# Seven block products instead of eight for five projections of the second attention, in a kernel of four fused layers

## The chip, the cores and the metric

One core of one Trainium2 chip runs the whole program. Its engines work side by side, each through its own list of instructions in order: TensorE (PE) multiplies, VectorE (DVE), ScalarE (ACT) and GpSimd (POOL) work element by element, SyncE (SP) issues DMAs. The metric is the device time of one execution in microseconds. Before the change the median of three runs was 269.13 (268.15 to 269.72).

## The reference, cut to what matters

Four layers follow one another on a sequence of 2048 tokens with 512 features: a linear attention, a feed-forward, and the same two again with the same weights. Each works on the layer norm of the running sum x and is added to it.

```python
def _A_ref(x, wqkv, wo):            # H = 32 heads of 16
    q, k, v = split(x @ wqkv)
    phi = lambda t: jnp.where(t > 0, t + 1, jnp.exp(t)) + 1e-6
    pq, pk = phi(q), phi(k)
    kv = einsum("bhsd,bhse->bhde", pk, v); z = einsum("bhsd->bhd", pk)
    o = einsum("bhqd,bhde->bhqe", pq, kv) / (einsum("bhqd,bhd->bhq", pq, z) + 1e-6)
    return o @ wo
def _B_ref(x, w1, w2):              # 512 -> 1376 -> 512
    return maximum(x @ w1, 0) @ w2
x = x + _A_ref(_layernorm(x), A_wqkv, A_wo)
x = x + _B_ref(_layernorm(x), B_w1, B_w2)
x = x + _A_ref(_layernorm(x), A_wqkv, A_wo)
x = x + _B_ref(_layernorm(x), B_w1, B_w2)
```

## The kernel before, in words

The 2048 tokens are 16 tiles of 128, in four chunks of four tiles. The running sum lies in xres, a tile's normalised rows in xn, their transposes (features down the partitions) in Tb. The transposes of the first six tiles are made on TensorE, all others by DMA, two tiles at a time (tr0_0 is the first half of chunk 0).

The program is written as a graph of named operations, each with its engine, what it reads and writes and a planned cost. `_list_schedule` puts them in an order per engine. An operation's priority is its place in the program plus an entry of the table HINTS; an entry with "!" fixes which of two engines does a flexible operation. The prefix is the layer (0 and 2 the attentions, 1 and 3 the feed-forwards). The table was found by a search, so layers overlap: the second attention's first chunks are worked on while the first feed-forward's last chunks still run. Every engine then follows its list in order and waits on semaphores.

**Attention.** For each chunk, K is computed in rows of tokens (`a_k`, kproj: four products of 128x512 per tile) and Q in rows of features (`a_q`, qproj: four products of 128x512 for each 128 features). So one chunk of either takes 16 products of 512 columns. `phi_evac` (lines 635 to 654) evicts each: on ScalarE a linear part with bias 1 + 1e-6 (_lin, L643) and an exponential (_exp, L645), both from PSUM, and on VectorE a minimum with 1 (_em, L647) and a maximum of the two parts (_phi, L653). `a_g` multiplies phi(K) with xn (g0, g1), `a_kv` with the V weights (kv), `a_m` masks by head (kvmask, L739) and multiplies with wo (m0 to m3), which ScalarE or VectorE evicts to Mf (mev0 to mev3, L746). The denominators go through `a_den`, logarithm and exponential, and a DMA that spreads them (spread); pqs (L801) applies them. The output tiles are Q times Mf (fin; the first four in two halves), added to xres by resid (L667) with the row sums, and sq (L675) gives the squares. A chain on GpSimd (mean, variance, power, L580 to L590) and a norm on VectorE or GpSimd (L601) or on ScalarE (L606) follow.

**Feed-forward.** Chunks 2 and 3 of the first and all chunks of the second already take the first product of the feed-forward in seven block products (`b_h7`), and all second products are taken so (`b_out`). The operands are cut in two both ways, sums of blocks are formed on VectorE (hs1 to hs4 at L900, usum, ssum, wsum), products h1 to h7 or p1 to p7 are run on TensorE, and the blocks of the result are put together in PSUM and on VectorE (hc11 and so on at L925, from a saved copy of a product that ScalarE makes at L938).

In the first attention the statistics come from bn_stats (L558), the inverse deviation from a logarithm and an exponential on ScalarE (lnv L564, rstd L566) or a power on GpSimd (L571), and the norm (fnorm, L596) from one of these:

```python
g.add_flex([(DVE, f, C_DVE_NORM_BF)] + ([(POOL, f, C_POOL_NORM)] if 0 < i < 8 else []),
           [("xin", i), ("mean", i), ("rstd", i)], [("xn", i)], name="fnorm%d" % i)
```

All matrix products have line 660, whatever they belong to; one is told from another by its operands.

LOCKED is a list of parts of names; the planner does not put an operation with such a name on VectorE at the same time as one on GpSimd:

```python
LOCKED = ("norm", "_em", "_phi", "pqs", "hs", "ssum", "usum", "wsum", "wvless", "madd")
```

## Time and profile before

| | |
|---|---|
| median of three runs | 269.13 us (268.15 to 269.72) |
| profiled execution | 268.56 us, its span 266.8 us |
| granted TensorE clock | 1.00 throughout |
| TensorE, products | 260.0 us busy, 1993 recorded |
| TensorE, weight loads | 181.8 us, 2008 |
| VectorE | 226.1 us |
| ScalarE | 185.8 us |
| GpSimd | 60.5 us |

The profile shows one execution. Rows of groups give a source line, engine, operation, output<-inputs and shape, the count behind x, then busy time in us and the mean of one in ns, then the idle time in front of them and what ended it. Rows of the timeline give start, duration, engine and line, and in brackets the idle time before. The chain of work is the line of releases followed back from the last instruction. Matmuls overlap each other and their ends are modelled, so a row's duration is longer than what the next one waits for. The program has 2008 products; a few records are missing.

### The profile page before, as it was taken

The page shows a single profiled execution, that of the slowest core. Times are in us where ns is not written, and L with a number is a line of the kernel's source. Part 1 is how long each engine was busy: PE and PEld are TensorE (multiplying, and loading weights), DVE is VectorE, ACT ScalarE, POOL GpSimd, SP SyncE. Part 2 cuts the span into 40 slices and gives each one's busy share as a digit, 9 for nine tenths or more (in the row PEclk, how much of TensorE's full clock was granted, in tenths as well). Part 3 has the DMA queues.
Part 4 walks back from the last instruction along what each step waited for, and adds up shares of the span by engine and source line. Part 5 has one row for each costly group of instructions (what it writes and reads, how often), then busy time and mean ns, then how long its engine had stood idle before and what let it go on. Part 6 is the DMA issues. An engine that isn't in the chain of part 4 may idle for free.

```text
span 266.8 us, 5440 instructions
## 1 busy us (share of the span) xinstructions
PE 260.0 (97%) x1993; PEld 181.8 (68%) x2008; DVE 226.1 (85%) x624; ACT 185.8 (70%) x407; POOL 60.5 (23%) x155
## 2 busy tenths in 40 slices
PE   7899999999999999999999999999999999999995
PEld 2555546545656798757778755764578698888884
DVE  5899974699997999899898777159998999899984
ACT  4799897876954148798945799588899945367400
POOL 4100000025672012550004540002645522000000
PEclk9999999999999999999999999999999999999999
DMA  6744297753584000522000460063483423400203
GB/s 197 275 122 87 52 273 270 174 136 63 93 119 90 2 20 4 98 41 42 0 2 0 79 82 0 2 154 84 80 121 76 42 54 87 79 2 20 81 37 122
DMA packets 45978, 22.44 MB, mean 84 GB/s; under 512 B 35872, under 2 KB 44416, under 8 KB 45952
## 3 DMA queue, kind: packets, MB, share of 16 engines
q1 hardware_dynamic: 45952, 22.09, 36.7%
q8 instruction: 16, 0.26, 0.5%
q14 instruction: 10, 0.08, 0.1%
HBM read 7.14 MB, written 2.10 MB: 35 GB/s over the span
## 4 chain that ended last, share of the span: by engine, by line
PE 83%; DVE 6%; DMA 4%; ACT 4%; SPq 1%; issue 1%; DVEq 0%
PE ps L660 83%; DVE xres L667 2%; DMA wqkv<-in_A_wqkv_dram 2%; DMA Tb<-xn 2%; ACT big L643 1%; ACT escr L645 1%; ACT Mf L746 1%; DVE xn L601 1%; SPq L477 1%; SPq L482 0%; DVE big L925 0%; DVE big L995 0%; DVE xn L995 0%; DVE Tb L995 0%; DVE big L801 0%
## 5 line engine op out<-in xcount | busy, mean ns | idle before, releaser
L643 ACT ACTIVATE big<-ps 128x512 bf16<-128x512 f32 x64 | 39.2, 648 | 6.4 <-PE ps L660 6.1
L675 ACT ACTIVATE sqscr<-xres 128x512 bf16<-128x512 f32 x48 | 30.1, 627 | 11.8 <-DVE xres L1097 6.6
L660 PE MATMUL ps<-Tb,w 128*128 128x256 f16 (+1 forms) x216 | 35.3, 304 | 0.4 <-DMA Tb<-xn 0.4
L660 PE MATMUL ps<-w,big 128*128 128x256 bf16 (+1 forms) x256 | 32.1, 272 | 0.0
L660 PE MATMUL ps<-Tb,wqkv 128*128 128x512 f16 (+1 forms) x144 | 31.8, 355 | 0.4 <-DMA wqkv<-in_A_wqkv_dram 0.3
L660 PE MATMUL ps<-big,xn 128*128 128x256 bf16 (+1 forms) x224 | 31.5, 288 | 0.0
L660 PE MATMUL ps<-wqkv,Tb 128*128 128x512 bf16 x119 | 29.6, 379 | 0.8 <-DMA wqkv<-in_A_wqkv_dram 0.4
L645 ACT ACTIVATE escr<-ps 128x512 bf16<-128x512 f32 x48 | 29.2, 637 | 0.8 <-PE ps L660 0.7
L660 PE MATMUL ps<-Mf,big 128*128 128x512 bf16 x125 | 28.8, 379 | 0.2
L660 PEld LDWEIGHTS ps<-big,xn 128*128 128x128 f16 x224 | 21.3, 98 | 9.0 <-issue 0.7
L660 PEld LDWEIGHTS ps<-w,big 128*128 128x128 bf16 (+1 forms) x256 | 24.8, 98 | 3.8 <-ACT big L976 0.3
L660 PEld LDWEIGHTS ps<-Tb,w 128*128 128x128 bf16 x216 | 20.8, 98 | 9.5 <-DMA Tb<-xn 0.7
L925 DVE TENSOR_TENSOR big<-ps,escr 128x512 bf16<-128x512 f32 (+1 forms) x40 | 23.6, 603 | 2.4 <-ACT escr L938 1.7
L938 ACT ACTIVATE escr<-ps 128x512 f32<-128x512 f32 (+1 forms) x40 | 20.8, 546 | 5.0 <-PE ps L660 3.8
L928 ACT ACTIVATE big<-big 128x512 bf16<-128x512 bf16 (+1 forms) x30 | 17.2, 581 | 10.0 <-DVE big L925 9.9
L647 DVE TENSOR_SCALAR escr<-escr 128x512 bf16<-128x512 bf16 x48 | 13.7, 288 | 11.6 <-ACT escr L645 11.4
L588 POOL TENSOR_TENSOR rstd<-veps,nhalf 128x2 f32<-128x2 f32 x24 | 18.9, 790 | 13.8 <-DVE veps L586 12.9
L660 PEld LDWEIGHTS ps<-Tb,wqkv 128*128 128x128 bf16 x144 | 13.9, 98 | 11.9 <-DMA wqkv<-in_A_wqkv_dram 0.5
L660 PEld LDWEIGHTS ps<-Mf,big 128*128 128x128 bf16 x128 | 12.3, 98 | 14.0 <-ACT Mf L746 0.4
L660 PEld LDWEIGHTS ps<-wqkv,Tb 128*128 128x128 f16 x128 | 12.2, 98 | 13.3 <-DMA wqkv<-in_A_wqkv_dram 0.9
L653 DVE TENSOR_TENSOR big<-big,escr 128x512 bf16<-128x512 bf16 x48 | 19.6, 419 | 0.7
L580 POOL TENSOR_SCALAR mean<-s 128x2 f32<-128x2 f32 x24 | 6.8, 283 | 54.4 <-DVE xres L667 53.3
(115 smaller groups left out, 522.0 us busy)
## 6 DMA issues: line engine op xcount, KB each, us to landing
big<-rdc SPq DMA_DIRECT2D x32, 128.0 KB, 2.7
xin<-in_A_x_dram SPq DMA_DIRECT2D x3, 512.0 KB, 6.7
w<-in_B_w_dram SPq DMA_DIRECT2D x1, 1376.0 KB, 8.2
w<-in_B_w_dram SPq DMA_DIRECT2D x1, 1280.0 KB, 11.3
wqkv<-in_A_wqkv_dram SPq DMA_DIRECT2D x4, 256.0 KB, 4.6
wqkv<-in_A_wqkv_dram SPq DMA_DIRECT2D x1, 512.0 KB, 5.0
wo<-in_A_wo_dram SPq DMA_DIRECT2D x1, 512.0 KB, 4.3
out_dram<-GT SPq DMA_DIRECT2D x1, 512.0 KB, 3.7
```

The costliest lines, as they stand in the source:

```text
L580: g.add(POOL, lambda e: e.tensor_scalar(mean[:, sl], s1[:, sl], -INV_D, None, ALU.mult), [("s1", i) for i in tl], [("mean", i) for i in tl ...
L588: g.add(POOL, lambda e: e.tensor_tensor(rstd[:, sl], veps[:, sl], nhalf[:, 0:n], ALU.pow), [("veps", lo), ("nhalf",)], [("rstd", i) for i ...
L643: g.add(ACT, lambda e: e.activation(dst_ap, psv[:, b, :], ACTF.Identity, bias=1.0 + 1e-6, scale=1.0), [("ps", b)], [dst_key], C_ACT_PSUM, ...
L645: g.add(ACT, lambda e: e.activation(sap, psv[:, b, :], ACTF.Exp), [("ps", b)], skeys, C_ACT_EXP, name=name + "_exp")
L647: g.add(DVE, lambda e: e.tensor_scalar(sap, sap, 1.0, 1e-6, ALU.min, ALU.add), skeys, skeys, C_DVE_BF4X, name=name + "_em")
L653: g.add(DVE, lambda e: e.tensor_tensor(dst_ap, dst_ap, sap, ALU.max), [dst_key] + skeys, [dst_key], 340.0, name=name + "_phi")
L660: last = e.matmul(o, l, r, start=st, stop=sp, skip_group_check=skip)
L667: g.add(DVE, lambda e: e.scalar_tensor_tensor(xres[:, i, :], psv[:, b, :], 0.0, src, ALU.add, ALU.add, accum_out=s1[:, i:i + 1]), [("ps", ...
L675: g.add(ACT, lambda e: e.activation(sqscr[:, q, :], xres[:, i, :], ACTF.Square, scale=math.sqrt(INV_D), accum_out=s2[:, i:i + 1]), xr(i), ...
L925: g.add(DVE, lambda e: e.tensor_tensor(ap, sh(psv[:, bank, 0:w]), sh(other()), ALU.add), [("ps", bank)] + okeys + ([] if first else bk), q ...
L928: g.add_flex([(ACT, lambda e: e.activation(ap, ap, ACTF.Relu), C_ACT_PSUM if len(cs) == 2 else 270.0), (DVE, lambda e: e.tensor_scalar(ap, ...
L938: g.add(ACT, lambda e, w=w: e.activation(q[:, 0:w], psv[:, bank, 0:w], ACTF.Identity), [("ps", bank)], key, C_ACT_PSUM if len(cs) == 2 els ...
```

## The change

In the second attention (layer 2), the K projection of chunks 1 and 2 and the Q projection of chunks 0 to 2 (list A7) are taken in seven block products. The chunk's Tb is cut into two pairs of tiles (tokens) and two pairs of feature blocks, the weights into two halves of input features and two of output features. `aw_sums` forms four weight sums per kind, eight operations on VectorE, into GT for K and Mf for Q, which are free then. `a7_sums` forms four token sums per chunk (as1 to as4), for chunks 0, 1 and 2, twelve operations on VectorE. `a7` runs seven products of four 128x256 matmuls each, so 28 of 256 columns take the place of 16 of 512. Three of the products are saved on ScalarE with the bias 1 + 1e-6 in them; three of the four result blocks are then sums of a PSUM bank and a saved one on VectorE (_add), the fourth is a linear part on ScalarE. For the three, the exponential reads the summed block from SBUF with a bias of -1 - 1e-6 (nbexp, a constant that GpSimd sets once) and not PSUM. Minimum and maximum stay, four each, now over two tiles' halves at a time.

The norms of tiles 1 to 7 in the first attention (fnorm) lose GpSimd as an alternative. In the order before, all 16 stand on VectorE. HINTS is replaced as a whole; a name that occurs twice in a layer now gets its own entry (#2). Nothing else in the graph changes. The new table changes which engine does flexible operations: of the 48 norms of layers 0 to 2, VectorE has 10 (20 before), ScalarE 26 (16), GpSimd 12 (12); of the first feed-forward's relus some go from VectorE to ScalarE.

Places where the two orders differ and which the text below speaks of, by operation names:

```
start, ScalarE        before: lnv0 rstd0 lnv1 rstd1          after: lnv0 lnv1 rstd0 rstd1
start, TensorE, up to the first product that reads the second half of Q's weights
                      before: trp0 trp1 kproj0 kproj1, four half-Q pieces, trp2 trp3
                      after:  trp0 trp1 kproj0 kproj1, three half-Q pieces, trp3 trp2
start, VectorE        before: ... veps5 fnorm7 fnorm4        after: ... bnag5 bnst8 fnorm4
loads, SP             before: tr1_1 wv0 tr2_0 tr2_1 wvl tr3_1 tr3_0 wo w1 w2a w2b
                      after:  tr1_1 wvl tr2_1 tr2_0 tr3_1 w2b tr3_0 wo w1 wv0 w2a
attention 2, ScalarE  before: q3_1_exp mev3 mev2 q3_1_lin q3_2_lin q3_2_exp
                      after:  q3_1_exp q3_1_lin q3_2_lin q3_2_exp mev2 mev3
attention 2, TensorE  after:  qproj3_2 m2 m3 fin0 fin1 fin3 (first halves) fin0 (second half)
```

The diff, cut to its core (HINTS left out):

```diff
+        self.seen = {}
...
+        self.seen[op.key] = self.seen.get(op.key, 0) + 1
+        op.key += "#%d" % self.seen[op.key] if self.seen[op.key] > 1 else ""
...
+        g.add(POOL, lambda e: e.memset(nbexp[:], -1.0 - 1e-6), [], [("nbexp",)], 100, name="ms_nbexp")
...
-                g.add_flex([(DVE, f, C_DVE_NORM_BF)] + ([(POOL, f, C_POOL_NORM)] if 0 < i < 8 else []),
+                g.add_flex([(DVE, f, C_DVE_NORM_BF)],
...
+        A7 = [('q', 0), ('q', 1), ('q', 2), ('k', 1), ('k', 2)]
...
+        def aw_sums(kind):
...
+            for (o, a, b, rd, k) in ((t1, b12, b11, [], 0), (t2, b22, t1, key(0), 1), (t3, b22, b12, [], 2), (t4, b21, t2, key(1), 3)):
+                f = (lambda e, o=o, a=a, b=b: e.tensor_tensor(o, a, b, ALU.subtract))
+                g.add_flex([(DVE, f, 340.0)], wk_ + rd, key(k), name="a%ssum%d" % (kind, k + 1))
...
+        def a7_sums(t):
...
+            for (o, a, b, op, rd, wr, nm) in ((s1_, a21, a22, ALU.add, kh, k1, "as1"), (s2_, s1_, a11, ALU.subtract, kl + k1, k2, "as2"),
+                                              (s3_, a11, a21, ALU.subtract, kl + kh, k3, "as3"),
+                                              (s4_, a12, s2_, ALU.subtract, kl + k2, k4, "as4")):
+                f = (lambda e, o=o, a=a, b=b, op=op: e.tensor_tensor(o, a, b, op))
+                g.add_flex([(DVE, f, 340.0)], rd, wr, name="%s_%d" % (nm, t))
...
+        def a7(kind, t):
...
+            def prod(n, bank, X, W, opens, reads):
+                def mk():
+                    mms = []
+                    for p in range(2):
+                        for d in range(2):
+                            x, w = (X[:, p, d, :], W[:, d, :]) if kind == "k" else (W[:, d, 128 * p:128 * p + 128], X[:, :, d, :])
+                            mms.append((psv[:, bank, 256 * p:256 * p + 256], x, w, opens and p == 0 and d == 0, d == 1, True))
+                    return mms
+                mm_group(mk, list(reads) + wk_, [("ps", bank)], 4 * C_MM256, "%s7_%d_%d" % (kind, t, n))
...
+                if v is None:
+                    g.add(ACT, lambda e: e.activation(dst, src(), ACTF.Identity, bias=1.0 + 1e-6, scale=1.0), [("ps", bank)], dk, C_ACT_PSUM, name=nm + "_lin")
+                else:
+                    g.add(DVE, lambda e: e.tensor_tensor(dst, src(), v[0], ALU.add), [("ps", bank)] + v[1], dk, C_DVE_PSUM, name=nm + "_add")
...
+                    g.add(ACT, lambda e: e.activation(sap, dst, ACTF.Exp, bias=nbexp[:, 0:1], scale=1.0), dk + [("nbexp",)], sk, C_ACT_EXP, name=nm + "_exp")
...
+            prod(1, BA, a11, b11, True, kl)
+            v1 = save(1, BA)
+            prod(2, BB, a12, b21, True, kl)
+            fin(11, 0, 0, BB, v1)
+            prod(5, BC, s1_, t1, True, k1 + key(0))
+            v5 = save(5, BC)
+            prod(6, BA, s2_, t2, False, k2 + key(1))
+            v6 = save(6, BA)
+            prod(3, BC, s4_, b22, False, k4)
+            fin(12, 0, 1, BC, v6)
+            prod(7, BA, s3_, t3, False, k3 + key(2))
+            fin(22, 1, 1, BA, v5)
+            prod(4, BA, a22, t4, False, kh + key(3))
+            fin(21, 1, 0, BA, None)
...
+                    if not first_layer and t == 0:
+                        for kind in "kq":
+                            if any(u == kind for u, _ in A7):
+                                aw_sums(kind)
+                    if not first_layer and any(u == t for _, u in A7):
+                        a7_sums(t)
+                    if not first_layer and ("k", t) in A7:
+                        a7("k", t)
...
+                    if not first_layer and ("q", t) in A7:
+                        a7("q", t)
+                    else:
+                        a_q(t, first=first_layer)
```

62 lines of the change are left out of this document (56 added, 6 removed), and 131 rows, old and new, of the table HINTS.

## The prediction

> **What bounds the kernel now.** I read the head of the page first, then the chain of work, then the matmuls in the timeline.
>
> ```profile
> span 266.8 us, 5440 instructions
> PE 260.0 (97%) x1993; PEld 181.8 (68%) x2008; DVE 226.1 (85%) x624; ACT 185.8 (70%) x407; POOL 60.5 (23%) x155
> ```
>
> A busy PE is a modelled row, so it proves little alone. The cadence does. The third column below is the time of the whole row, xN its instructions.
>
> ```profile
> 119.88 1.47 PE L660 MATMUL ps<-xn,xin 128*128 128x256 f16 x12
> 189.28 2.76 PE L660 MATMUL ps<-Mf,big 128*128 128x512 bf16 x12
> 205.09 58.75 PE ps L660 x539
> L660 PE MATMUL ps<-Mf,big 128*128 128x512 bf16 x125 | 28.8, 379 | 0.2
> L660 PE MATMUL ps<-Tb,w 128*128 128x256 f16 x152 | 21.0, 272 | 0.4 <-DMA Tb<-xn 0.4
> L660 PEld LDWEIGHTS ps<-Tb,w 128*128 128x128 bf16 x216 | 20.8, 98 | 9.5 <-DMA Tb<-xn 0.7
> ```
>
> One 512-column product takes 379 ns from start to end, yet twelve take 2.76, so one starts every (2.76 - 0.38) / 11 = 0.216 us. A 256-column one starts every (1.47 - 0.27) / 11 = 0.109. The chain holds 539 products in one piece of 58.75 us, again 0.109 each, nothing between. A weight load takes 98 ns, less than 109, so it hides. TensorE is really full, and the time is the count of its columns plus the holes in its stream. The holes:
>
> ```profile
> 4.18 5.93 DMA wqkv<-in_A_wqkv_dram
> 7.05 1.47 PE L660 MATMUL ps<-wqkv,Tb 128*128 128x512 bf16 x6 [0.38 <-DMA wqkv<-in_A_wqkv_dram]
> 10.16 0.61 PE L660 MATMUL ps<-Tb,wqkv 128*128 128x256 f16 x4 [0.32 <-DMA wqkv<-in_A_wqkv_dram]
> 125.01 0.39 PE L660 MATMUL ps<-xn,w 128*128 128x256 f16 x2 [0.15 <-ACT lnd L938]
> 198.94 0.61 PE L660 MATMUL ps<-Tb,w 128*128 128x256 f16 x4 [0.43 <-DMA Tb<-xn]
> ```
>
> The bracket counts from the modelled end of the product before. Against the cadence add 0.27 - 0.11 = 0.16: 0.31 us is lost at 125.0 and 0.6 at 198.9. Up to 10.16 TensorE waits for weights.
>
> **The products themselves.** Five projections (K of chunks 1, 2, Q of chunks 0 to 2) each trade 16 products of 512 columns for 28 of 256. Removed: 80 x 0.216 = 17.28. Added: 140 x 0.109 = 15.26. **-2.02 us**, on the path. Were the 98 ns loads to show, it would be nothing.
>
> **What VectorE pays.** Durations (columns as above; the last number before the bar is the mean of one, in ns):
>
> ```profile
> L925 DVE TENSOR_TENSOR big<-ps,escr 128x512 bf16<-128x512 f32 x28 | 18.9, 684 | 2.4 <-ACT escr L938 1.7 <-ACT big L955 0.6
> L900 DVE TENSOR_TENSOR xn<-Tb 128x512 f16<-128x512 f16 x12 | 4.9, 418 | 0.0
> L601 DVE TENSOR_SCALAR xn<-xres,mean,rstd 128x512 f16<-128x512 f32 x20 | 11.1, 562 | 0.1
> L606 ACT ACTIVATE xn<-xres,nbias,rstd 128x512 f16<-128x512 f32 x16 | 12.9, 813 | 5.3 <-POOL nbias L590 2.9 <-DVE nbias L590 2.3
> L977 DVE TENSOR_SCALAR big<-ps 128x512 bf16<-128x512 f32 x9 | 6.0, 686 | 0.1
> L596 DVE TENSOR_SCALAR xn<-xin,mv,rstd 128x512 f16<-128x512 bf16 x16 | 5.9, 408 | 0.7 <-ACT rstd L566 0.7
> 110.00:150.00 40.00, 39.64 (x300) 29.34 (x303) 36.36 (x114) 29.71 (x67) 10.94 (x32) 1.00 0.14 25
> 150.00:180.00 30.00, 29.89 (x210) 18.40 (x210) 15.87 (x51) 24.87 (x52) 4.87 (x13) 1.00 0.37 70
> ```
>
> Each projection adds three PSUM-plus-saved sums (like L925): 15 x 0.684 = 10.3. Twelve sums of tokens and eight of weights (like L900): 20 x 0.418 = 8.4. ScalarE keeps eight operations per projection (three saves and one linear part for four linear parts). The new order moves 10 norms from VectorE to ScalarE (10 x 0.562 = 5.6 off, 10 x 0.813 = 8.1 on), and three relus of the first feed-forward (3 x 0.686 = 2.1 off) with some smaller ones. VectorE nets about +8 us, ScalarE about +9.
>
> Room: in the two rows of stretches (columns PE, PEld, DVE, ACT, POOL) VectorE is busy 52.2 of 70 us. The new work lands mostly there: +18.7, less some 7 of norms and relus, makes about 64 of 68. It fits on the whole, but 110 to 150, at 36.4 of 40, is nearly full before anything is added. There I followed VectorE's new sequence by hand: from the first sums of chunk 2 it works without a break, and the third block sum of the feed-forward's chunk 2 ends about 0.2 us after its product (p7) could start. Taken: +0.2; bounds 0 and +1.4 (two of the 0.68 evictions in front of it). The 0.31 at 125.0 belongs to an order that is gone: **-0.3** (0 if one like it returns).
>
> **First tiles' norms.** All 16 L596 norms are on VectorE already, none is on GpSimd: keeping them off it changes nothing. Nor does the added memset, on an idle GpSimd. What changes at the start is order. Before 10.16 TensorE now has three half-Q pieces to do instead of four, so one, 2 x 0.109 = 0.22 us, is left behind the weights that land then. The first tile's inverse deviation now stands behind the second tile's logarithm on ScalarE: some 0.6 us later, but the product behind it waits for weights until 7.05 anyway. Tile 4's norm comes behind one more statistics operation, about 0.1 late. **+0.3** (0 to 0.7).
>
> **The V weights' load** goes from before the late transposes to behind w1 on the DMA queue:
>
> ```profile
> 34.04 0.58 SPq L507 DMA_DIRECT2D wo<-in_A_wo_dram  x1
> w<-in_B_w_dram SPq DMA_DIRECT2D x1, 1376.0 KB, 8.2
> w<-in_B_w_dram SPq DMA_DIRECT2D x1, 1280.0 KB, 11.3
> 44.15 0.28 PE L660 MATMUL ps<-GT,wqkv 128*128 128x128 bf16 x2
> ```
>
> w1 is issued at 34.66 and lands 8.2 later, at 42.9; w2 at 35.23 lands at 46.5, so 1280 KB take 3.6 us in turn. Issued between them, 512 KB take 1.4 and land near 44.3, or 43.9 if the norms in front of the queue run some 0.4 earlier, as the new order has it. VectorE then subtracts (0.42), with everything behind it held. The product that needs it (44.15 before, some 0.7 later in the new order) is reached near 44.9. Taken: **+0.2**, bounds 0 and +1.0 (the load 1 us late).
>
> **Second attention's end.** ScalarE spaces its 512-wide evictions by 0.49:
>
> ```profile
> 159.57 0.49 ACT escr L645
> 160.06 0.49 ACT big L643
> ```
>
> The last two evictions of the folded output matrix now stand behind both operations of the last Q block. From that block's end: a hand-over of about 0.15, 4 x 0.49 = 1.96, another of 0.1: 2.2 us. TensorE reaches the product that needs them after two matrix products and three half output tiles, 8 x 0.216 = 1.73. **+0.5** (0 to 0.8).
>
> **Second feed-forward's start.** The hole at 198.9 is a transpose issued late:
>
> ```profile
> 194.64 4.25 DMA Tb<-xn
> ```
>
> It lands 4.25 later. In the new order its norm stands further ahead of its first reader (about 4.4 us of products between issue and reader, 3.7 before): **-0.6** (-0.6 to 0).
>
> **Sum:** -2.02 - 0.3 + 0.3 + 0.2 + 0.2 + 0.5 - 0.6 = -1.7. The joints of a new order that I did not follow I price at +0.2 (0 to 2: the two holes above are what a searched order leaves in 250 us, several such would be 2). **-1.5 us.** The profiled execution took 268.56 (266.8 span and 1.8 around it), 0.57 under the median 269.13; the forecast for the median is **267.6**.
>
> One rule speaks against a gain. GpSimd's norms here run 766 ns at best, but beside a two-input VectorE sum:
>
> ```profile
> L601 POOL TENSOR_SCALAR xn<-xres,mean,rstd x12: 766/772/1566, 62.5 to 223.7; 128x512 f16<-128x512 f32 x12
> 118.86 1.57 POOL L601 TENSOR_SCALAR xn<-xres,mean,rstd 128x512 f16<-128x512 f32 x1
> 119.87 1.23 DVE L995 TENSOR_TENSOR big<-big 128x1280 bf16<-128x1280 bf16 x1
> 118.94 0.81 DVE L995 TENSOR_TENSOR xn<-Tb,big 128x1280 bf16<-128x1280 bf16 x1
> ```
>
> The norm takes 0.8 longer and one sum 0.4 longer (1.23 for 0.81). The twelve token sums carry none of the names (LOCKED) that keep such pairs apart. GpSimd is busy 15.8 of the 70 us, so some three of twelve would meet it: 3 x 0.4 = 1.2 on VectorE, which has the room. I take 0 for it. The Trainium skill, "SBUF — State Buffer", "Who interferes with whom", says that the two engines hold the shared port pair for a whole instruction and the other blocks fully; the trace agrees (1.57 for 0.77). Were all of that on the path the sum would be -0.3.
>
> **Rivals.** (1) *No measurable change*: of -2.0, more than 1.0 more goes into holes than I count: the V load 1 us late, or three new holes of 0.3 to 0.6 like the two shown. For it: every stage is packed so that a hole of 0.3 is normal. Time 268.7. (2) *Slower*: VectorE becomes the bound between 110 and 150. Its 36.4 of 40 carries 8 to 10 us more when the weight sums, the first Q chunk and the K chunk all fall there, before its relus come off; each microsecond past 40 is waited for, since feed-forward sums and attention evictions feed TensorE in turn. It decides once VectorE's work in that stretch passes about 43 us: then 3 us of holes outweigh the gain. At 44.5, 4.5 us late: 269.1 - 1.5 + 4.5 = 272. Against it: at 85% over the span VectorE has met every deadline but two. The Trainium skill, "Perfetto Trace Analysis", "Identifying the Most-Contended Engine", says not to judge TensorE by matmul busy time but by arithmetic use and weight-load share. By that rule TensorE (68%) is behind VectorE (85%) and this change loads the wrong engine; the 0.109 cadence in the trace says otherwise. (3) *The products save nothing*, because twice as many weight loads show: 269.5; the 98 under 109 makes this unlikely.
>
> **How the numbers follow.** About 0.5% (1.35 us) is what a measurement can tell from no change, so -1.5 is only just a gain. Faster by more (under 267.8): 0.51. Within: 0.32, rival 1 and half of rival 3 (0.02 of it). Slower by more: 0.17, rival 2. The forecast's own range is 266.1 (the holes of before gone, nothing new: -2.9) to 268.6 (the V load and one more hole). The range for all is 265.9 to 270.8; beyond it above lies most of rival 2.
>
> **What would show it.** Right: 2068 matmuls for 2008, the 256-column cadence at 0.109 in the new products, no L596 on GpSimd, new block sums of 0.42 and 0.68. Each step has its hole: a wait on weights near 44 us, on ScalarE's last matrix evictions before the output tiles, on VectorE between 110 and 150, none near 198. Wrong: VectorE over 95% between 100 and 150 with TensorE waiting for it, GpSimd norms of 1.5 us often, or holes of over 1 us at the transposes.

## The result, and the profile after

The change made the kernel slower. The median of 20 runs is 270.60 us (269.35 to 271.69), against 268.85 (268.01 to 270.51) for 20 runs of the kernel before: a ratio of 1.0059, with a 95% interval of 1.0043 to 1.0076, or some 1.6 us. The forecast was 267.6. Runs of one kernel differ by up to 2.5 us, and one profile is one run: the profile after took 271.26 (span 269.5), 0.66 over its median, the profile before 0.3 under its own.

The head of the page after, with TensorE's share as before and the busy times of the others up:

```profile
span 269.5 us, 5611 instructions
PE 261.7 (97%) x2052; PEld 188.0 (70%) x2068; DVE 233.9 (87%) x645; ACT 196.3 (73%) x424; POOL 61.2 (23%) x153
PE 78%; ACT 10%; DVE 4%; DMA 4%; issue 1%; POOL 1%; DVEq 0%
```

2068 weight loads for 2008, as forecast; VectorE is up by 7.8 us and ScalarE by 10.5 (forecast +8 and +9).

To compare two streams of products I give each product its full cadence (0.216 us for 512 columns, 0.109 for 256, 0.056 for 128), add these up in the kernel's order, and subtract the sum from the time at which the product really starts, counted from the first warm-up product at 1.24. What is left is TensorE's lost time up to that product. The products come to 256.2 us before and 254.2 after, 2.0 less. The lost time is 6.1 before and 10.8 after. A few records are missing, so a single figure is good to about 0.2. By stretch of product time (the stretch that begins at 110 begins near 118 on the clock after), rounded:

| lost us in | first 20 | 20-64 | 64-110 | 110-125 | 125-160 | 160-180 | 180-210 | rest |
|---|---|---|---|---|---|---|---|---|
| before | 3.4 | 0.7 | 0.0 | 0.5 | 0.1 | 0.2 | 1.2 | 0.2 |
| after | 5.2 | 1.2 | 0.0 | 1.3 | 0.9 | 1.4 | 0.7 | 0.2 |

So +4.7 lost and -2.0 saved make the 2.7 between the two profiles. Outside the first 20 us three of these losses are steady: in every profile with the changed kernel's own order, those of the experiments below included, 110-125 loses 0.8 to 2.0 and 160-180 1.4 to 2.5, and 20-64 loses 1.2 to 1.7 in all but the four with the edit a_tr. Where it is lost, from the timeline of TensorE after (the bracket is idle time and what ended it; the third number is the time of the whole row):

```profile
5.51 0.61 PE L631 MATMUL ps<-ident,xn 128*128 128x128 f16 x4 [0.67 <-DVE xn L602]
6.81 2.74 PE L666 MATMUL ps<-wqkv,Tb 128*128 128x512 bf16 x6
9.34 0.97 PE L666 MATMUL ps<-Tb,wqkv 128*128 128x256 f16 x4
12.41 0.82 PE L666 MATMUL ps<-wqkv,Tb 128*128 128x512 bf16 x2 [0.35 <-ACT Tb L637]
71.27 1.47 PE L666 MATMUL ps<-Tb,w 128*128 128x512 f16 x8 [0.35 <-DMA Tb<-xn]
124.31 1.49 PE L666 MATMUL ps<-w,big 128*128 128x256 bf16 x12 [0.16 <-ACT big L1059]
127.57 0.83 PE L666 MATMUL ps<-xn,w 128*128 128x256 f16 x6 [0.23 <-ACT lnd L1042]
132.18 0.61 PE L666 MATMUL ps<-wqkv,Tb 128*128 128x256 bf16 x4 [0.19 <-ACT big L1059]
154.88 1.05 PE L666 MATMUL ps<-wqkv,Tb 128*128 128x256 bf16 x8 [0.41 <-DMA Tb<-xn]
```

At the start six products of 512 columns take 2.74 us, where before they took 1.47: TensorE runs at half cadence up to about 10 us. There is a new hole at 71, three behind ScalarE between 124 and 132, one behind a transposed load at 154.9. The new products run as forecast: eight in 1.05 are one per 0.11. The hole of before near 199 is gone. (In a_start and a_tr, below, 0.4 to 0.6 is lost at its place again.) In the same two stretches as the prediction quoted (columns PE, PEld, DVE, ACT, POOL), VectorE and ScalarE are both fuller:

```profile
110.00:150.00 40.00, 39.28 (x335) 32.03 (x336) 38.69 (x110) 34.30 (x75) 11.37 (x29) 1.00 0.09 17
150.00:180.00 30.00, 29.44 (x240) 21.46 (x241) 21.89 (x71) 26.32 (x52) 5.83 (x16) 1.00 0.25 38
```

VectorE has 38.7 of 40 us between 110 and 150 (36.4 before), ScalarE 34.3 (29.7). The chain of waits says which of the two stands in front of TensorE there. Before, it leaves TensorE at 117.5 for VectorE and comes back at 125.0 by way of two ScalarE operations:

```profile
111.66 5.81 PE ps L660 x33
117.49 0.43 DVE big L957
123.33 0.70 DVE big L925
124.68 0.28 ACT lnd L938
```

After, it leaves TensorE at 113.5 for ScalarE and stays with it, but for a chain on GpSimd from 125.9 to 128.8, until 132.2:

```profile
113.50 0.60 ACT big L649
126.53 1.16 POOL veps L592
131.65 0.49 ACT big L1059
132.18 10.91 PE ps L666 x98
```

From 113.5 to 128.0 ScalarE is busy 14.5 of 14.5 us in this trace, VectorE 13.8. The waits on ScalarE behind the holes at 124 and 127.6 lie in that stretch.

At the second attention's end the chain after passes through VectorE from 180.5 to 183.8:

```profile
173.68 6.83 PE ps L666 x67
180.53 0.69 DVE GT L836
181.81 0.67 DVE big L909 x2
183.80 6.47 PE ps L666 x30
```

Before, the chain leaves TensorE at 178.25 too, for ScalarE and then VectorE, but on the way to the transposed load of the hole at 198.9 (its row of 194.64 stands in the prediction); TensorE itself lost only 0.2 in 160-180.

```profile
161.58 16.65 PE ps L660 x131
178.25 0.60 ACT escr L645
182.31 0.43 DVE big L653
```

### The profile page after: what moved, and what is told of

Its sections match the earlier page's. It is cut to its first block, busy times and chain, and to the rows that moved or that the text cites. A ratio compares the mean times of both kernels' runs of the same rounds, so it can differ in the third digit from the quotient of the medians.

```text
span 269.5 us, 5611 instructions
## 1 busy us (share of the span) xinstructions
PE 261.7 (97%) x2052; PEld 188.0 (70%) x2068; DVE 233.9 (87%) x645; ACT 196.3 (73%) x424; POOL 61.2 (23%) x153
## 4 chain that ended last, share of the span: by engine, by line
PE 78%; ACT 10%; DVE 4%; DMA 4%; issue 1%; POOL 1%; DVEq 0%
PE ps L666 77%; DMA Tb<-xn 3%; ACT sqscr L681 2%; ACT big L649 1%; ACT xn L612 1%; DVE big L1029 1%; ACT escr L778 1%; ACT escr L651 1%; DMA xin<-in_A_x_dram 1%; ACT big L1032 1%; ACT rdc L893 1%; ACT lnd L891 1%; PE ps L631 1%; ACT escr L753 1%; DVE xres L673 1%
## 5 line engine op out<-in xcount | busy, mean ns | idle before, releaser
L666 PE MATMUL ps<-big,xn 128*128 128x256 bf16 (+1 forms) x221 | 32.1, 287 | 0.2
L649 ACT ACTIVATE big<-ps 128x512 bf16<-128x512 f32 x44 | 27.4, 652 | 3.2 <-PE ps L666 3.1
L666 PE MATMUL ps<-wqkv,Tb 128*128 128x512 bf16 (+1 forms) x106 | 26.3, 378 | 1.2 <-DMA Tb<-xn 0.4
L666 PE MATMUL ps<-Tb,wqkv 128*128 128x512 f16 (+1 forms) x120 | 24.0, 334 | 0.1
L1042 ACT ACTIVATE escr<-ps 128x512 f32<-128x512 f32 (+1 forms) x40 | 20.3, 553 | 4.4 <-PE ps L666 4.1
L666 PEld LDWEIGHTS ps<-Mf,big 128*128 128x128 bf16 x128 | 12.0, 98 | 14.5 <-DVE big L909 1.4
L612 ACT ACTIVATE xn<-xres,nbias,rstd 128x512 f16<-128x512 f32 x26 | 20.9, 817 | 0.6 <-POOL nbias L596 0.5
L651 ACT ACTIVATE escr<-ps 128x512 bf16<-128x512 f32 x28 | 17.5, 632 | 1.9 <-PE ps L666 1.9
L586 POOL TENSOR_SCALAR mean<-s 128x2 f32<-128x2 f32 x24 | 7.5, 311 | 49.3 <-DVE xres L673 46.5
L666 PEld LDWEIGHTS ps<-wqkv,Tb 128*128 128x128 f16 x112 | 10.6, 100 | 10.9 <-issue 0.8
L666 PE MATMUL ps<-xn,w 128*128 128x256 f16 x120 | 17.5, 273 | 0.2 <-ACT lnd L1042 0.2
L666 PE MATMUL ps<-w,Tb 128*128 128x96 bf16 (+2 forms) x176 | 17.4, 224 | 0.0
## 6 DMA issues: line engine op xcount, KB each, us to landing
big<-rdc SPq DMA_DIRECT2D x32, 128.0 KB, 2.7
```

What stands on the lines that cost most here:

```text
L586: g.add(POOL, lambda e: e.tensor_scalar(mean[:, sl], s1[:, sl], -INV_D, None, ALU.mult), [("s1", i) for i in tl], [("mean", i) for i in tl ...
L612: (ACT, lambda e: e.activation(xn[:, i, :], src, ACTF.Identity, scale=rstd[:, i:i + 1], bias=nbias[:, i:i + 1]), C_ACT_SB_AP)],
L649: g.add(ACT, lambda e: e.activation(dst_ap, psv[:, b, :], ACTF.Identity, bias=1.0 + 1e-6, scale=1.0), [("ps", b)], [dst_key], C_ACT_PSUM, ...
L651: g.add(ACT, lambda e: e.activation(sap, psv[:, b, :], ACTF.Exp), [("ps", b)], skeys, C_ACT_EXP, name=name + "_exp")
L666: last = e.matmul(o, l, r, start=st, stop=sp, skip_group_check=skip)
L1042: g.add(ACT, lambda e, w=w: e.activation(q[:, 0:w], psv[:, bank, 0:w], ACTF.Identity), [("ps", bank)], key, C_ACT_PSUM if len(cs) == 2 els ...
```

## The experiments

Most edits move single operations. They are made on the planner's finished order, and the waits are worked out anew from the moved order; all else stays. The diffs below show an engine's list of operations before and after such a move. "rstd", "norm" and so on carry the tile's number. Lost time is that of each kernel's own profile, counted as above; "over the changed kernel" is the difference of the two ratios to the kernel before.

### The start: order, idle time and clock

```diff
 ScalarE, first tiles (changed kernel; a_start)
-lnv0, lnv1, rstd0, rstd1
+lnv0, rstd0, lnv1, rstd1
 VectorE
-stats1, fnorm0, fnorm1
+fnorm0, stats1, fnorm1
```

> The changed kernel with one thing put back: the first tile's inverse deviation stands ahead of the second tile's logarithm on ScalarE again, and the first tile's norm ahead of the second tile's statistics on VectorE. Theory 1 (clock): in the changed kernel TensorE idles 1.1 us after its warm-up products instead of 0.4, and then runs at half cadence (128 columns in 106 ns, 512 in 427) up to 10.0 us. With the gap back at 0.4 the full cadence (56 and 216 ns) comes from about 4.8 us on, the start gives back 1.8 us: 268.8 us, ratio to the kernel before 1.000. Rival (the first products only moved, since the weights that land near 10 us set the end of the start anyway): nothing changes, 270.6, ratio 1.006, with full cadence or without it. My prediction's own price of the start (0.3) would give 270.3, 1.005.

b_start makes the opposite swap in the kernel before; a_fill changes one line, in the changed kernel:

```diff
-                for k in range(WARM):
+                for k in range(WARM + 2):
```

> The kernel before with the reverse edit: the second tile's logarithm stands ahead of the first tile's inverse deviation on ScalarE, and the second tile's statistics ahead of the first tile's norm on VectorE. Theory 1 (clock): the first transposes come some 0.7 us later, the idle time after the warm-up products grows to about 1.1 us, the cadence halves up to about 10 us and the kernel before gets 1.3 to 1.8 us slower: ratio 1.005 to 1.007. Rival (weights set the end of the start anyway): ratio 1.000 to 1.001.

> The changed kernel with ten warm-up products of 512 columns instead of eight, everything else in the same order. The two more take 0.85 us in the gap of 1.1 us before the first transposes, so nothing is held up by them. Theory 1 (idle time costs the clock): full cadence from about 5.5 us on, 1.5 to 1.8 us gained, about 269.0, ratio 1.001. Rival (the order of the first tiles itself costs the time, not the clock): no change, 270.6, ratio 1.006; or slower by up to 0.3 if the warm-up ends late.

Measured: a_start 269.51, ratio 1.0031 (1.0007 to 1.0055); b_start 268.41, ratio 0.9991 (0.9968 to 1.0013); a_fill 270.43, ratio 1.0063 (1.0040 to 1.0085). The clock theory, that the wide gap costs 1.8 us, falls: the kernel before with the wide gap lost nothing, and the filled gap gained nothing. The profiles say why: at the start the same order is fast in one execution and slow in the next. This is a_norm (below), whose start is that of the changed kernel instruction for instruction:

```profile
5.47 0.40 PE L631 MATMUL ps<-ident,xn 128*128 128x128 f16 x4 [0.64 <-DVE xn L602]
6.56 1.47 PE L666 MATMUL ps<-wqkv,Tb 128*128 128x512 bf16 x6 [0.24 <-ACT Tb L637]
9.43 0.61 PE L666 MATMUL ps<-Tb,wqkv 128*128 128x256 f16 x4 [1.40 <-DMA wqkv<-in_A_wqkv_dram]
11.46 0.83 PE L666 MATMUL ps<-Tb,wqkv 128*128 128x256 f16 x6 [0.33 <-DMA wqkv<-in_A_wqkv_dram]
```

Full cadence at once, with the same idle time ahead, and then 1.4 us of waiting for the Q weights: the first Q pieces start at 9.43, and at half cadence, in the profile after, they started at 9.34. Half cadence up to about 10 us came in four of the twelve profiles with the wide gap and in none of the eight with a narrow or filled one. The gap may make it likelier, but these are too few to tell, and the medians show no cost. The Trainium skill, "TensorE: Matmul & The Clock Gate", Part 1, says that the clock rises at the end of a window that runs freely, so that the same kernel starts differently from run to run; these traces agree: 2.74 and 1.47 us for the same six products.

The order itself is worth something less certain: a_start is 0.0028 under the changed kernel, 0.75 us, but the two intervals overlap, and the profiles do not bear it out. The four with this edit (a_start, a_all, a_best, a_cover) lost 4.2 to 5.4 in the first 20 us, the other twelve of the changed order 3.3 to 5.4.

### What the saved columns are worth

a_eight issues the first block product of each projection twice, 20 more matmuls of 256 columns (the second pass opens the sum again):

```diff
-                    return mms
+                    return mms + mms if n == 1 else mms
```

> The changed kernel in which the first of the seven products of each of the five projections is issued twice into an open sum (20 more products of 256 columns, 2.18 us of TensorE; the first time it opens the bank, the second time it opens it again, so the sum is the same). It asks what columns are worth there. If TensorE is the bound all through the second attention, as the prediction had it, all of it shows: 2.2 us over the changed kernel, 272.8, ratio 1.014. Theory 2 (between 112 and 155 us TensorE waits for ScalarE, or for VectorE by the prediction's rival): most of the products fall where there is slack, and 0.5 to 1.5 us show: 271.1 to 272.1, ratio 1.008 to 1.012.

Measured: 272.57, ratio 1.0138 (1.0103 to 1.0174), 0.0079 or 2.1 us over the changed kernel, for 2.18 us of added columns; the ends of the two intervals allow 0.7 to 3.5. Its profile has a start at half cadence like that of the changed kernel, and its span is 2.0 us longer (271.5 for 269.5) with the same lost time in all, though not in the same places. So, as near as can be told, all of it shows: the 2.0 us saved are real too, and no slack on TensorE was found in the second attention into which they could vanish.

### 110 to 135 us: ScalarE or VectorE

a_saves takes work off ScalarE, a_sums off VectorE (both leave part of the computation out), a_relu moves it from the one to the other, a_norm from ScalarE to GpSimd, a_two joins a_norm and a_sums.

```diff
 a_saves
-activation(q, psv[:, bank, :], Identity, bias=1.0 + 1e-6)
+activation(q[:, 0:32], psv[:, bank, 0:32], Identity, bias=1.0 + 1e-6)
 a_sums
-tensor_tensor(o, a, b, op)                                   # 20 block sums
+tensor_scalar(o, a, 1.0, 0.0, ALU.mult, ALU.add)
-tensor_scalar(sap, sap, 1.0, 1e-6, ALU.min, ALU.add)         # 15 clamps
+tensor_scalar(sap[:, :, 0:32], sap[:, :, 0:32], 1.0, 1e-6, ALU.min, ALU.add)
 a_relu: nine relus (hc22r_2_4 to hc22r_3_4)
-ScalarE
+VectorE, each behind its sum
 a_norm: norm5, norm6, norm9, norm10 of the second attention
-ScalarE
+GpSimd, behind the statistics
```

> The changed kernel with ScalarE's fifteen saves of block products (three per projection) narrowed from 512 to 32 columns; the rest of the saved sums stays what lay there before, so part of the computation is left out. It takes about 15 x 0.3 = 4.5 us off ScalarE, nothing off VectorE. Theory 2 (ScalarE's queue, full from 113.5 to 132, holds up the second attention): the holes between 120 and 133 us and the one at 154 close for the most part, 1.0 to 2.0 us gained: 268.6 to 269.6, ratio to the kernel before 0.999 to 1.003. Rival (VectorE is the bound in that stretch, 43.5 of 45 us busy): not over 0.4 us, 270.2 to 270.6, ratio 1.005 to 1.006. Rival (joints of the new order, transposes issued late): nothing.

> The changed kernel with VectorE lightened: its twenty block sums are copies of their first operand (one input instead of two, about 0.13 us less each) and the fifteen clamps behind the exponentials of block tiles are 32 columns wide (0.2 us less each), so part of the computation is left out. About 5 us off VectorE, all but 1 us of it between 105 and 190 us; nothing off ScalarE. Rival (the prediction's: VectorE is the bound between 110 and 150): 1.0 to 2.0 us gained, 268.6 to 269.6, ratio 0.999 to 1.003. Theory 2 (ScalarE): not over 0.4 us, ratio 1.005 to 1.006.

> The changed kernel with nine relus of the first feed-forward's last two chunks (those of the summed blocks, 112 to 135 us) moved from ScalarE to VectorE, each right behind its sum: some 3.8 us off ScalarE, 1.6 to 2 us on VectorE, which is 43.5 of 45 us busy there. Theory 2 (ScalarE is the bound): 0.5 to 1.5 us gained, 269.1 to 270.1, ratio 1.001 to 1.004. Rival (VectorE is the bound): 0.5 to 2 us slower, 271.1 to 272.6, ratio 1.008 to 1.014.

> The changed kernel with four norms of the second attention's stretch (tiles 5, 6, 9 and 10) moved from ScalarE to GpSimd, behind the statistics there: 3.3 us off ScalarE, 3.1 to 6.3 us on GpSimd (12.3 of 45 us busy; 0.77 us each, 1.57 beside a two-input sum), VectorE untouched but for the sums it meets there. Theory 2 (ScalarE): 0.5 to 1.5 us gained, ratio 1.001 to 1.004. Rival (VectorE): no gain, and up to 0.8 us slower through four meetings with sums at 0.2 to 0.4 each, ratio 1.006 to 1.009.

> The changed kernel with both engines lightened at once: the four norms of tiles 5, 6, 9, 10 on GpSimd instead of ScalarE (3.3 us off ScalarE), and the twenty block sums as copies and the fifteen clamps narrowed on VectorE (about 5 us off; part of the computation is left out). Each alone left 1.1 to 1.3 us of lost TensorE time between 110 and 135 us in the profile. Theory 4 (both engines are full there, and lightening one leaves the other): together 0.6 us or less is lost there, 269.0 or less, ratio to the kernel before at most 1.002. Rival (fixed latencies of the joints, which no lighter engine shortens): 1.1 to 1.3 us lost there as before, ratio 1.004 to 1.006.

| kernel | median us | ratio (95%) | lost 110-125 | lost 125-160 |
|---|---|---|---|---|
| changed | 270.60 | 1.0059 (1.0043 to 1.0076) | 1.3 | 0.9 |
| a_saves | 269.84 | 1.0042 (1.0022 to 1.0062) | 1.2 | 0.7 |
| a_sums | 269.70 | 1.0037 (1.0015 to 1.0059) | 1.2 | 0.2 |
| a_relu | 271.92 | 1.0097 (1.0066 to 1.0129) | 2.0 | 0.9 |
| a_norm | 271.08 | 1.0068 (1.0044 to 1.0093) | 1.1 | 1.0 |
| a_two | 270.19 | 1.0047 (1.0029 to 1.0066) | 0.9 | 0.6 |

VectorE alone is out: a_sums takes 1.3 us off it between 110 and 150, and the three holes behind ScalarE stay, 0.3 to 0.4 each. ScalarE is not tested by a_saves as it was meant to be: only two of the fifteen narrowed saves run between 113.5 and 128, where ScalarE is still busy 14.0 of 14.5 us, and all three holes stay. a_norm moves tile 5's norm out of that stretch; the hole at 124 closes and that at 132 shrinks from 0.35 to 0.15 or less, but others open behind VectorE, of 0.2 near 122 and of 0.6 near 153. So the sums of the table hardly move. Off both, 0.4 less is lost in 110-125, which is between the two expectations. The times of a_saves, a_sums, a_norm and a_two cannot be told from the changed kernel's: the intervals overlap. In a_relu, nine relus more on VectorE cost 1.0 us of time, with intervals that overlap too, and 0.7 of lost time, and most of the releasers in its timeline change from ScalarE to VectorE:

```profile
126.00 0.83 PE L666 MATMUL ps<-xn,w 128*128 128x256 f16 x6 [0.24 <-ACT lnd L1042]
130.57 1.05 PE L666 MATMUL ps<-wqkv,Tb 128*128 128x256 bf16 x8 [0.20 <-DVE big L1029]
132.23 0.72 PE L666 MATMUL ps<-w,big 128*128 128x256 bf16 x5 [0.39 <-DVE big L1099]
140.03 1.49 PE L666 MATMUL ps<-w,big 128*128 128x256 bf16 x12 [0.40 <-DVE big L771]
```

So VectorE had little room left there, but it was ScalarE that stood in front of the changed kernel's three holes. For the one at 127.57, which stays at 0.4 us in all six kernels, this is what ScalarE does just ahead of it (changed kernel, timeline):

```profile
125.61 0.71 ACT L1042 ACTIVATE escr<-ps 128x512 f32<-128x512 f32 x1
126.09 0.94 ACT L612 ACTIVATE xn<-xres,nbias,rstd 128x512 f16<-128x512 f32 x1
126.80 0.72 ACT L1042 ACTIVATE lnd<-ps 128x512 f32<-128x512 f32 x1
```

Tile 4's norm stands in front of the eviction that TensorE waits for. This gave a third theory, of single operations in the way.

### Single operations in the way

```diff
 a_joint
-ScalarE: norm5, exp, sq7, ... hc21_2_4, ... norm4, hv5_3_2, ... norm6
+ScalarE: exp, sq7, ... hc21_2_4, norm5, ... hv5_3_2
+GpSimd: nbias4, norm4, ... nbias6, norm6
 a_tr: VectorE, first feed-forward
-nbias2, resid7, resid12, norm2
+nbias2, norm2, resid7, resid12
 a_end: second attention's end
-VectorE: kvmask0, gev1_0, mev1, pqs0_3     ScalarE: rdc1, mev0
+VectorE: kvmask0, pqs0_3                   ScalarE: rdc1, gev1_0, mev0, mev1
 a_all: these three and a_start
```

> The changed kernel with three norms of the second attention's stretch taken out of the way of what the next product waits for: tile 5's on ScalarE goes from in front of four evictions to behind the last relu of the feed-forward's chunk 2, tiles 4 and 6 go from ScalarE to GpSimd. Theory 3 (joints: a few single operations stand in front of the one that TensorE waits for, while the engines' totals have room): the holes at 123.9 (0.42 us), 127.1 (0.5) and 131.7 (0.36) close, 0.8 to 1.3 us of TensorE's lost time between 110 and 135 us are gone, 269.3 to 269.8, ratio to the kernel before 1.0015 to 1.0035. Rival (engine totals: VectorE and ScalarE are both full there): the holes move on to the next products and under 0.4 us is gained, ratio 1.004 to 1.006.

> The changed kernel with one norm of the first feed-forward's first chunk (tile 2, on VectorE) two output tiles earlier, 1.3 us, so that the second transposed load of that chunk is issued 1.3 us earlier. Theory 3: the hole of 0.5 us at 70.5, where the product waits for this load, closes, 270.1, ratio 1.004. Rival (the residual sums that now come 0.5 us later hold up their banks): nothing, ratio 1.006 to 1.007.

> The changed kernel with two evictions at the second attention's end (the last of the folded key-value matrix and the second of the folded output matrix, 0.68 us each on VectorE) back on ScalarE, where the kernel before has them. Theory 3: VectorE's chain from 180.5 to 183.7, on which the product for the mask at 183.1 and the first output tiles wait, is 1.2 us shorter, and 0.4 to 0.7 us of the 1.2 us lost between 172 and 188 come back: 269.9 to 270.2, ratio 1.0035 to 1.005. My prediction's step (ScalarE's last two evictions set the end): nothing or 0.3 us slower, since ScalarE gets two more in front of them, ratio 1.006 to 1.007.

> The changed kernel with the edits of the last three runs and the first tile's inverse deviation and norm ahead of the second tile's again. Theory 3: the parts add up, 0.8 to 1.3, 0.4 to 0.7 and 0.5, and 0.75 for the start as measured: 267.3 to 268.3, ratio 0.994 to 0.998, faster than the kernel before. Rival (engine totals, or holes that move on): 269.0 to 270.0, ratio 1.001 to 1.005.

a_tr: 269.57, ratio 1.0047 (1.0029 to 1.0065), and its profile has no hole any more at that place:

```profile
69.00 1.46 PE L666 MATMUL ps<-Tb,w 128*128 128x512 f16 x8
70.30 0.50 PE L666 MATMUL ps<-w,Tb 128*128 128x96 bf16 x8
70.64 2.54 PE L666 MATMUL ps<-Tb,w 128*128 128x512 f16 x14
```

The lost time of 20-64 went from 1.2 to 0.6, and it is 0.6 to 0.8 in all four profiles with this edit (a_tr, a_all, a_best, a_cover). The time follows by 0.3 with overlapping intervals. So the cause of this hole is shown by the profiles: a late transposed load, behind a norm that stood behind two residual sums.

a_joint: 271.07, ratio 1.0094 (1.0070 to 1.0118), 0.0035 over the changed kernel with overlapping intervals, and no gain. The holes at 124 and 132 closed, but others of 0.2 to 0.6 opened at the products in between (one on ScalarE's eviction, now behind tile 5's norm; one on VectorE, which had waited 0.5 for ScalarE). Lost in 110-125: 1.7. The theory falls for this stretch, in this form: neither place tried for this norm of 0.8 us in ScalarE's list was harmless.

a_end: 270.54, ratio 1.0085 (1.0062 to 1.0109). No gain; the product at the mask now waits for VectorE, and VectorE for ScalarE:

```profile
180.49 0.29 DVE L653 TENSOR_SCALAR escr<-escr 128x512 bf16<-128x512 bf16 x1 [0.66 <-ACT escr L651]
180.70 0.42 DVE L847 TENSOR_TENSOR KVT<-ps,bmask 128x256 bf16<-128x256 f32 x1
181.18 0.60 PE L666 MATMUL ps<-wo,KVT 128*128 128x512 bf16 x2 [0.42 <-DVE KVT L847]
```

a_all: 270.18, ratio 1.0070 (1.0043 to 1.0097): the parts do not add up, since two of them are no gains.

### The second attention's end

a_end2 takes a_end and puts the mask and one scaled Q tile ahead of the last Q block on VectorE, and the last two matrix evictions ahead of it on ScalarE. a_cover brings back the order on TensorE that the kernel before has there:

```diff
 a_end2, on top of a_end
-VectorE: q3_1_em, kvmask1, q3_1_phi, pqs0_1     ScalarE: q3_2_lin, q3_2_exp, mev2, mev3
+VectorE: kvmask1, pqs0_1, q3_1_em, q3_1_phi     ScalarE: mev2, mev3, q3_2_lin, q3_2_exp
 a_cover, on top of a_best
-TensorE: qproj3_2, m2, m3, fin0_0 ... fin3_2, den3, fin2_0 ... fin8_0
+TensorE: m2, m3, qproj3_2, fin0_0 ... fin3_2, fin2_0 ... fin8_0, den3
 (VectorE and ScalarE nearly as in a_end2, the two evictions of a_end left on VectorE)
```

> The changed kernel with the two evictions at the second attention's end back on ScalarE, and in addition the second mask product of the key-value matrix and the second scaled Q tile ahead of the last Q block's clamp on VectorE, and the last two evictions of the folded output matrix ahead of the last Q block's on ScalarE. Theory (the order of VectorE in front of the mask, not the number of its evictions, sets the end): the hole at the mask product (0.25 in the changed kernel, 0.63 with the evictions moved alone) closes and 0.4 to 0.9 us come back there, ratio 1.001 to 1.004. Rival (the end's products are too few to cover the chain in any order): the loss moves to the first output tiles and the denominators behind them, ratio 1.005 to 1.008.

> The changed kernel with the three edits of the last run on it (tile 2's norm in the first feed-forward, the first tile's norm, the K product ahead of the Q pieces), and with the second attention's end covered as in the kernel before: on TensorE the last Q projection goes from in front of the two matrix products to behind them, and the last denominator to behind the first six output tiles; on VectorE the second mask product and two scaled Q tiles go ahead of the last Q block's clamp; on ScalarE the last two matrix evictions go ahead of the last Q block's. Theory (the end lacks products to cover VectorE's and ScalarE's chain): 0.5 to 0.9 of the 1.1 to 1.2 us lost between 172 and 188 us come back: 268.2 to 268.6, ratio to the kernel before 0.997 to 0.999. Rival (the chain is VectorE's and as long in any order): the loss stays over 0.8 us, ratio 1.000 to 1.003.

a_end2: 271.91, ratio 1.0122 (1.0094 to 1.0150), slower by 1.7 us than the changed kernel. The hole at the mask closed, and the loss came back larger further on, at the last denominator and the output tiles of chunk 1:

```profile
182.34 0.59 PE L666 MATMUL ps<-wo,KVT 128*128 128x512 bf16 x2
182.77 2.75 PE L666 MATMUL ps<-Mf,big 128*128 128x512 bf16 x12
185.87 0.40 PE L666 MATMUL ps<-big,Zc 128*32 128x512 bf16 x4 [0.35 <-DVE big L659]
188.09 2.12 PE L666 MATMUL ps<-Mf,big 128*128 128x512 bf16 x9 [0.86 <-DVE big L909]
```

a_cover: 276.63, ratio 1.0290 (1.0255 to 1.0326). It tells nothing of the end, since I broke something else: with the last denominator later, the DMAs that spread its result come later, and the next layer's transposed loads stand behind them on SP's queue:

```profile
192.50 2.50 SPq L903 DMA_DIRECT2D big<-rdc  x4
195.14 3.16 SPq L617 DMA_TRANSPOSE Tb<-xn  x2
198.38 4.02 PE L666 MATMUL ps<-Tb,w 128*128 128x256 f16 x18 [3.74 <-DMA Tb<-xn]
```

In the changed kernel these two loads are issued at 191.84. What the second attention's end would cost in the old order of its products stays open.

### The hole at 199 of the kernel before, the best of the edits, and the order as a whole

```diff
 b_tr: kernel before, second feed-forward, chunk 1
-VectorE: resid10, veps4, ... resid11, veps6, norm5     ScalarE: sq9, hv1_0_0, norm4
+VectorE: veps4, resid10, ... norm5, resid11, veps6     ScalarE: norm4, sq9, hv1_0_0
 a_best: a_start and a_tr, and on TensorE
-kproj0_0, kproj0_1, kproj1_0, qh0_0_3_0, qh0_0_2_0, kproj1_1
+kproj0_0, kproj0_1, kproj1_0, kproj1_1, qh0_0_3_0, qh0_0_2_0
 a_old
-HINTS = {...}     # the changed kernel's
+HINTS = {...}     # the kernel before's
```

> The kernel before with three small operations of the second feed-forward's second chunk earlier (one variance step ahead of a residual sum, two norms ahead of a residual sum and of an eviction), so that the transposed load for which TensorE waits 0.6 us at 198.9 is issued some 1.0 us earlier. My prediction's term of -0.6 for this hole: 268.0, ratio 0.997 to 0.998, faster than both kernels. Rival (what was moved back becomes late in turn): ratio 1.000 or more.

> The changed kernel with the norm of tile 2 of the first feed-forward earlier, the first tile's inverse deviation and norm ahead of the second's, and on TensorE the last K product of tile 1 ahead of the first Q pieces, which in seven of ten profiles waited 0.6 to 1.6 us for their weights while that product waited behind them. If the parts add up (0.3 to 0.5, 0.75 and up to 0.4): 268.9 to 269.3, ratio 1.000 to 1.002. If the start is set by the landing of the weights alone: the last part gives nothing, ratio 1.002 to 1.003.

> The changed kernel with the kernel before's table of order corrections (priorities and engine choices by operation name), so that the block products, their sums and saves stand where the planner puts them without a search. It parts the change in two: what the products and their evictions bring in an order that was made for other work, and what the new search brings. If the products fit in easily: 267 to 269. My theory now (VectorE and ScalarE have no room to spare in the second attention, and it is the search that fits the new work in): 1 to 6 us slower than the changed kernel, 271.5 to 276.5, ratio 1.010 to 1.029.

b_tr: 268.74, ratio 0.9996 (0.9978 to 1.0014). In its profile the hole is gone (lost in 180-210: 0.5 for 1.2), but a gain of 0.5 us is not to be seen in the time, nor excluded. No version was found that measurably beats the kernel before.

a_best: 269.11, ratio 1.0006 (0.9994 to 1.0019). Three edits, of two, one and one operations, bring the changed kernel level with the one before: 0.0053, 1.4 us. The intervals are apart. The start's wait for weights was still 1.2 us in its profile, so the K product ahead of the Q pieces did not remove it.

a_old: 284.66, ratio 1.0618 (1.0565 to 1.0671), 15 us over the changed kernel, far more than I expected. In its page the chain passes through VectorE for 13%:

```profile
span 281.6 us, 5614 instructions
PE 68%; DVE 13%; DMA 7%; ACT 7%; SPq 2%; issue 1%; POOL 0%; DVEq 0%
```

The seven products in an order that was made for other work are a loss many times their saving; the new order takes most of it back, and stops short.

## Why the prediction was right or wrong

- **The products, -2.02: right.** 256.2 us of columns became 254.2, cadence 0.11, and in a_eight added columns there cost about their full time. Rival 3 is out.
- **The start, +0.3: too small, and its cause stays open.** The profiles show 5.2 lost for 3.4 before, but a start differs by up to 2 us from run to run in one and the same order, so this pair of profiles says little. Over all profiles the first 20 us lost 4.7 on average in the sixteen of the changed order (3.3 to 5.4), and 3.5, 4.2 and 4.3 in the three of the order before: some 0.7 more, from few profiles. My sentence that the later first norm is hidden because "the product behind it waits for weights until 7.05 anyway" did not hold in the profile after, where that product starts at 6.81 without a wait for weights. The piece left behind the weights was seen: the second group of Q pieces waits for them in ten of the sixteen profiles with the changed order.
- **First tiles' norms kept off GpSimd, 0: right.** All 16 are on VectorE in both.
- **V weights, +0.2: not there.** No wait for them appears near 44 to 46; the stretch 20-60 loses 0.5 after and 0.6 before.
- **VectorE 110 to 150, +0.2, and the hole at 125 gone, -0.3: this is a step that failed.** The stretch 110-125 lost 0.8 more instead of 0.1 less. I followed VectorE's list by hand and not ScalarE's, to which I had just given 9 us, "ScalarE about +9", without a price. The three holes there wait for ScalarE, which is busy without a break from 113.5 to 128. The hole of 125.0 came back with them: at 127.57 the same kind of product waits for the same kind of eviction (L938 before, L1042 after), 0.4 for 0.3. The bound of +1.4 contains the size, but it was worked out for a wait on VectorE.
- **Rival 2, VectorE full: half right.** The sign I had named was over 95% between 100 and 150 with TensorE waiting for it. VectorE has 47.4 of 50 us there, 94.7%, just under it (46.1 before), and TensorE waits for ScalarE; lightening VectorE (a_sums) did not close the holes. Over the two stretches it has 60.6 us of work, not the 64 that I had counted. But it has little room: work moved off ScalarE to it (a_relu), or ScalarE's norms taken away (a_norm), let VectorE be what TensorE waits for next. How much each would cost alone, no run says.
- **Second attention's end, +0.5 (0 to 0.8): mis-sized.** 160-180 lost 1.2 more, over the upper bound. I had named ScalarE's last two evictions; the chain of waits runs over VectorE from 180.5 to 183.8. Neither order of these chains that was tried gave it back, so the cause stays open.
- **Second feed-forward's start, -0.6: right in the profile.** 180-210 lost 0.7 for 1.2, a gain of 0.5. It is not in every profile: a_start and a_tr wait for that load again. b_tr closes the same hole in the kernel before, without a measurable gain in time.
- **Joints not followed, +0.2 (0 to 2): this is the other step that failed.** The hole at 71 costs 0.5 (shown by a_tr). The one at 154.9 costs 0.6 in this profile. Of the others with the same order around it, a_saves and a_all have it and a_start, a_tr, a_fill and several more do not, so it comes and goes with the execution.
- **GpSimd beside VectorE, 0: nothing in the runs speaks against it.**

Put together from the profiles, without the start: -2.0 and, by the table, +0.5, +0.8, +0.8, +1.2 and -0.5 make +0.8; with some 0.7 for the start 1.5, where 1.6 was measured. That this comes so near is partly luck, since 0.6 of it is the hole at 154.9, which most profiles do not have. The gain of 2.0 was not lost in one place. It went into steady losses of 0.5 to 1.2 in three places (behind a late transposed load at 71, behind ScalarE at 110-125, and at the second attention's end), a fourth that comes and goes, and the start.

## What to carry to other kernels

Where TensorE is full, as here, saved columns are worth about their full time, but the evictions and sums that pay for them go to engines that release TensorE's next products: price each of these engines by its own list, and not only the one that looks fullest. In a hand-ordered or searched program no edit is local: a norm of 0.8 us moved out of one product's way stood in front of an eviction for another, and a denominator moved behind six output tiles held up a queue of DMAs that served another layer. Small terms of a forecast should be compared with the spread of one profile (here 2 us at the start alone) before a single trace is read for them.

## What the runs showed of the hardware

- In the first 10 us TensorE's cadence is half or full by the execution and not by the kernel alone: six 512-column products took 2.74 us in the profile after and 1.47 in a_norm, with the same instructions. The granted clock of the page shows 1.00 in both.
- The landing of the same weights, issued at the same times, differs by 1.7 us and more between executions: the first Q piece waited 1.4 us for them in a_norm and started at 9.43; in a_relu it started at 7.75, in a_tr at 7.91, without a wait.
- Over the first 20 us of products the profiles lost between 3.3 and 5.4 us, and this goes with the time of the run. Of the sixteen profiles of the changed order, the four that lost 4.0 or less there took 0.3 to 1.3 us less than their kernel's median; the twelve that lost 4.2 or more took up to 1.6 us more, none less.
